# Attention inside a fused attention and two-MoE kernel: projections by float32 matmuls of 64 rows in place of float32r matmuls of a split chunk

## The chip, the cores and the metric

The kernel runs as one program on one core of a Trainium2 chip. The metric is the time of one execution on the device, in microseconds (us), lower is better. PE is the matmul engine (PEld its weight loads), DVE the vector engine, ACT the scalar engine, POOL the GpSimd engine, SP the engine whose queue issues the DMAs.

## What is computed

Three stages follow one another. The first is attention with random features; its output is the input of a gated feed-forward layer (moe1), and that one's output goes through a mixture of eight experts with balanced weights (moe2). The change touches the attention alone:

```
batch, n_heads, seq, head_dim = (4, 8, 576, 64);  n_features = 128
scale = 1.0 / np.sqrt(np.sqrt(D));  q_s, k_s = (q * scale, k * scale)
def phi(x):
    proj = np.einsum('bhsd,md->bhsm', x, omega)
    sq = np.sum(x * x, axis=-1, keepdims=True) / 2.0
    h = proj - sq
    h = h - np.max(h, axis=-1, keepdims=True)
    return np.exp(h) / np.sqrt(m)
q_p, k_p = (phi(q_s), phi(k_s))
kv = np.einsum('bhsm,bhsd->bhmd', k_p, v);  z = np.sum(k_p, axis=2)
num = np.einsum('bhsm,bhmd->bhsd', q_p, kv)
den = np.einsum('bhsm,bhm->bhs', q_p, z)[..., None] + 1e-06
return num / den
```

All arrays are float32.

## The kernel before

The attention works on 36 chunks (18 of k, 18 of q, in turn; `chunks` in `attention`), each of eight blocks of 128 tokens of one head. Every chunk comes from memory twice: as `c["x"]`, tokens in the partitions, and as `xt`, the turned chunk, in which partitions 0 to 63 hold one head's 64 dimensions and partitions 64 to 127 another's. A chunk goes through stages, and the table `ORDER` says in which order the stages are written in each step of the loop `for step in range(NCH + 8)` and how many steps after the chunk's number each stage comes. Each engine runs its instructions in the order in which they were written; nothing reorders them later. So a step is one round of the table, in which every engine handles pieces of several chunks.

- `s0`, `s0r`, `s0n`: sum of squares of a chunk: three POOL instructions (L492, L494, L495) into one scratch block `t0[:, 3]`, one reduction on DVE (L501), a scaling on POOL (L507) to `nsq`. The scratch block is single, so the squares of the next chunk wait for the reduction of this one.
- `s1a`, `s1b`: the turned chunk is split in a high float32r part (ACT, L477) and a low one (DVE, L481).
- `s2p`: the projection on PE. The weights `bdh`, `bdl` are block diagonal, so that one matmul of 128 rows and 256 columns gives two heads; with the split it takes three matmuls (L529, L530, L531) for each of four blocks, 12 for a chunk, into two PSUM banks.
- `s2m`, `s2b`, `s2c`: on DVE the maxima, one reduction for each of the two banks (L536), then two small instructions of 128x8, `hm` (L540) and `bi` (L544).
- `s2x`: on ACT eight exponentials of 128x128 (L551).
- `s3`, `s3a`: for a k chunk, kv and z by ten float32 matmuls of 66 columns (L566, L567), copied out by ACT (L580); for a q chunk eight transposes (L571), copied out by ACT (L584).
- `s4`, `s4d`, `s4r`, `s4n`: q chunks only: eight float32 matmuls of 66 columns (L600; for the tails of the sequence 16 of 64 rows of output, L598), and on DVE denominator (L612), reciprocal (L617) and product (L622).
- `s5`, `s5a`, `s5b`: q chunks only: four transposes (L632), then the output as a high part (ACT, L643) and a low part (DVE, L648).
- `pump`: one piece of the conversion of moe1's first weights (on DVE, POOL and ACT), two pieces in a step.

PSUM has eight banks; `RINGS` says which banks a use takes in turn. In the attention `tr3` has banks 0 and 3, and `tr5`, `pr` and `nu` share six banks. `moe1` is a generator of which each step from NCH + 2 = 38 on takes one piece, so that its matmuls begin in step 38, while the attention's last stages drain. From there on the rings are `DRAIN`.

Of the kernel before, what the change touches and what calls it, by code (L numbers as in the profile page):

```python
# [50 lines left out]
class Kernel:  # L51
    def __init__(self, tc, x, v, vt, omega, wg, wv, wo, w2g, w1, w2, out):
# [10 lines left out]
    ORDER = [("s3a0", 4), ("s0r", 0), ("s5a", 8), ("s2p0", 2), ("s1a", 1), ("s2m0", 2), ("s2p1", 2), ("s40", 5),  # L63
# [3 lines left out]
    RINGS = dict(tr3=(0, 3), tr5=(4, 5, 6, 7, 2, 1), pr=(4, 5, 6, 7, 2, 1), nu=(4, 5, 6,  # L67
                 7, 2, 1), a=(0, 1, 2, 3), b=(4, 5, 6, 7))

    DRAIN = dict(RINGS, tr3=(4, 5), tr5=(4, 5), nu=(6, 7))  # L70

# [289 lines left out]
    def run(self):  # L361
        tc, nc = self.tc, self.nc
        with ExitStack() as ctx:
# [7 lines left out]
            upper = ExitStack()  # L371
            psum = upper.enter_context(tc.tile_pool(name="upper", bufs=1, space=PSUM))
            self.banks += [psum.tile([P, 512], F32, tag=f"b{i}", name=f"bank{i}") for i in range(4, 8)]
# [12 lines left out]
            with tc.manual_schedule():  # L386
                m1 = self.moe1()
                self.attention(m1)
                for _ in m1:
                    pass  # L390
                rest = self.moe2()
                upper.close()
# [6 lines left out]
    def attention(self, m1):  # L399
        tc, nc = self.tc, self.nc  # L400
        if True:
# [7 lines left out]
            t6 = af.tile([P, 2, 2, M], F32R, tag="t6", name="at6")  # L409
# [7 lines left out]
            om2 = t3[:, 0, 0:M]  # L417
            bdh, bdl = t6[:, 0], t6[:, 1]
            nc.gpsimd.memset(f(t6), 0.0)
# [7 lines left out]
            xts = [bx[:, i * 512:(i + 1) * 512] for i in range(4)]  # L427

# [15 lines left out]
            def load(i):  # L444
# [6 lines left out]
                for w, t in ((1, xt), (0, t0[:, k])):  # L451
# [16 lines left out]

            def s1(i):
                c = st[i]  # L470
                k = turn("xT", 4)
                c["xh"], c["xl"] = [self.ar2[:, (x * 4 + k) * 512:(x * 4 + k + 1) * 512].rearrange("p (a t) -> p a t", t=P) for x in range(2)]
                c["tr"] = c["xt"].rearrange("p (a t) -> p a t", t=P)

            def s1a(i):
                c = st[i]
                nc.scalar.copy(c["xh"], c["tr"])  # L477

            def s1b(i):
                c = st[i]  # L480
                nc.vector.tensor_tensor(c["xl"], c["tr"], f(c["xh"]), op=ALU.subtract)  # L481
# [28 lines left out]
            def s2(i):  # L510
# [4 lines left out]
                else:  # L515
                    e = t1[:, turn("e", 2)].rearrange("p (a m) -> p a m", m=M)
                c["e"] = e
                mx = sm.tile([P, 8], F32, tag="mx", name=f"mx{i}", bufs=4)
                hm = sm.tile([P, 8], F32, tag="hm", name=f"hm{i}", bufs=4)
                bi = sm.tile([P, 8], F32, tag="bi", name=f"bi{i}", bufs=4)  # L520
                c["mx"], c["hm"], c["bi"], c["pr"] = mx, hm, bi, []

            def s2p(i, u):
                c = st[i]
                xh, xl = c["xh"], c["xl"]
                pr = self.bank("pr", 2, 2 * M)
                for w in range(2):
                    a = 2 * u + w
# [3 lines left out]
                c["pr"].append(pr)  # L532

            def s2m(i, u):
                c = st[i]
                nc.vector.reduce_max(c["mx"][:, 4 * u:4 * u + 4], c["pr"][u].rearrange("p w (h m) -> p (w h) m", m=M), axis=AX.X)  # L536

            def s2b(i):
                c = st[i]
                nc.vector.scalar_tensor_tensor(c["hm"], c["mx"], SCALE, c["nsq"], op0=ALU.mult, op1=ALU.add)  # L540
# [5 lines left out]
            def s2x(i, u):  # L546
                c = st[i]
                e, bi = c["e"], c["bi"]
                for a in range(4 * u, 4 * u + 4):
                    pr = c["pr"][a // 4].rearrange("p w (h m) -> p (w h) m", m=M)  # L550
                    nc.scalar.activation(e[:, a, :], pr[:, a % 4, :], AF.Exp, bias=bi[:, a:a + 1], scale=SCALE)  # L551
# [100 lines left out]
            fns = dict(s0=s0, s0r=s0r, s0n=s0n, s1=s1, s1a=s1a, s1b=s1b, s2=s2, s2b=s2b, s2c=s2c, s4r=s4r, s5=s5, s5a=s5a, s5b=s5b, pump=pump)  # L652
            halves = dict(s2p=s2p, s2m=s2m, s2x=s2x, s3=s3, s3a=s3a, s4=s4, s4d=s4d, s4n=s4n)
# [11 lines left out]
            for h in range(2):  # L665
                r = slice(h * D, (h + 1) * D)
                nc.scalar.copy(bdh[r, h, :], om2[r])
# [886 lines left out]
```

## Time and profile before

| | |
|---|---|
| time of the runs, median (lowest to highest of 3) | 2108.16 us (2104.68 to 2111.72) |
| the profiled execution: own time given as the span from first to last instruction | 2106.0 us |
| PE busy in the span | 2059.6 us (98%) |
| DVE busy | 1401.3 us (67%) |
| POOL busy | 1053.9 us (50%) |
| ACT busy | 825.8 us (39%) |
| mean granted clock of TensorE | 0.996 |

Busy times are sums over the whole program. Matmuls are pipelined and their ends are modelled, so a PE that reads as busy is not PE at its peak; the distance from the start of one instruction to the start of the next tells more. The program has stages with different limits, and the attention is only the first 180 us of it, so the shares above say little about it. Which of the listed runs was the profiled one is not recorded.

### The profile page before, as it was taken

What the parts mean: (1) busy time and instruction counts of PE and PEld (TensorE: products, weight loads), DVE (VectorE), ACT (ScalarE), POOL (GpSimd) and SP (SyncE); (2) the same over time, 40 slices, a digit from 0 to 9 for tenths busy, and PEclk for the clock granted to TensorE, in tenths of its full rate; (3) what the DMA queues carried; (4) which work ended last, traced back from release to release, by engine and by line L of the source; (5) the groups of instructions that cost most, each with busy time, mean ns of one, the idle gap of its engine ahead of it and who ended that gap; (6) DMA issues with size and microseconds to landing.
All of it is one profiled execution on the core that took longest, in us unless ns stands there. A gap on an engine that the chain in (4) does not pass through costs nothing.

```text
span 2106.0 us, 32639 instructions
## 1 busy us (share of the span) xinstructions
PE 2059.6 (98%) x11836; PEld 1997.4 (95%) x11836; DVE 1401.3 (67%) x2321; ACT 825.8 (39%) x1843; POOL 1053.9 (50%) x1047
## 2 busy tenths in 40 slices
PE   7899999999999999999999999999999999999998
PEld 6889999999998889989888999999999999999998
DVE  6997678778755645445445666666688666666666
ACT  6786433333334444334333423323233433323322
POOL 6783656656533455455652543434454543443443
PEclk9999999999999999999999999999999999999999
DMA  6552556555424656766768788777888887887784
GB/s 203 162 162 77 179 165 197 172 182 176 136 85 157 235 216 228 267 228 246 267 228 303 249 258 264 260 258 251 297 264 267 273 263 258 261 264 253 247 274 153
DMA packets 238130, 467.78 MB, mean 222 GB/s; under 512 B 20272, under 2 KB 110096, under 8 KB 233872
## 3 DMA queue, kind: packets, MB, share of 16 engines
q1 hardware_dynamic: 237968, 465.68, 66.7%
q8 instruction: 94, 1.54, 0.3%
q14 instruction: 68, 0.56, 0.1%
HBM read 340.25 MB, written 125.35 MB: 221 GB/s over the span
## 4 chain that ended last, share of the span: by engine, by line
PE 90%; DVE 7%; POOL 1%; issue 1%; DMA 1%; ACT 0%; SPq 0%; DVEq 0%; POOLq 0%; ACTq 0%
PE bank L1079 13%; PE bank L1325 7%; PE bank L1327 7%; PE bank L1326 7%; PE pair L1416 7%; PE pair L1418 7%; PE pair L1417 7%; PE bank L723 5%; PE bank L725 5%; PE bank L724 5%; PE bank L1020 4%; PE bank L1022 4%; PE bank L1021 3%; PE bank L755 2%; PE bank L757 2%; PE bank L756 2%
## 5 line engine op out<-in xcount | busy, mean ns | idle before, releaser
L1428 DVE TENSOR_TENSOR sums<-pair,sums 128x768 f32<-128x768 f32 x209 | 198.8, 951 | 44.3 <-PE pair L1418 44.3
L1325 PE MATMUL bank<-xh,ar 128*128 128x384 f32 x564 | 188.7, 335 | 2.4 <-ACT mt L1358 2.1
L1327 PE MATMUL bank<-xh,ar 128*128 128x384 f32 x564 | 188.4, 334 | 0.0
L1326 PE MATMUL bank<-xl,ar 128*128 128x384 f32 x564 | 188.4, 334 | 0.0
L1095 DVE SCALAR_TENSOR_TENSOR ac<-bank,mt,ac 128x512 f32<-128x512 f32 x84 | 63.1, 751 | 131.2 <-PE bank L1079 129.3
L1416 PE MATMUL pair<-xh,ar 128*128 128x384 f32 x344 | 115.0, 334 | 0.2 <-DVE sums L1428 0.2
L1418 PE MATMUL pair<-xh,ar 128*128 128x384 f32 x344 | 114.9, 334 | 0.0
L1417 PE MATMUL pair<-xl,ar 128*128 128x384 f32 x344 | 114.9, 334 | 0.0
L1325 PEld LDWEIGHTS bank<-xh,ar 128*128 128x128 f32 x564 | 105.9, 188 | 3.4 <-ACT mt L1358 2.7
L1326 PEld LDWEIGHTS bank<-xl,ar 128*128 128x128 f32 x564 | 105.9, 188 | 0.0
L1327 PEld LDWEIGHTS bank<-xh,ar 128*128 128x128 f32 x564 | 105.9, 188 | 0.0
L737 ACT CAST ar<-mt 128x384 fp32r<-128x384 f32 x72 | 37.0, 514 | 172.6 <-DVE mt L734 172.6
L723 PE MATMUL bank<-xh,ar 128*128 128x384 f32 x288 | 96.6, 336 | 0.0
L725 PE MATMUL bank<-xh,ar 128*128 128x384 f32 x288 | 96.2, 334 | 0.0
L725 PE MATMUL bank<-xh,ar1b 128*128 128x384 f32 x288 | 96.2, 334 | 0.0
L724 PE MATMUL bank<-xl,ar 128*128 128x384 f32 x288 | 96.2, 334 | 0.0
L723 PE MATMUL bank<-xh,ar1b 128*128 128x384 f32 x288 | 96.2, 334 | 0.0
L724 PE MATMUL bank<-xl,ar1b 128*128 128x384 f32 x288 | 96.2, 334 | 0.0
L551 ACT ACTIVATE at<-bank,bi 128x128 f32<-128x128 f32 x288 | 78.4, 383 | 44.5 <-DVE bi L544 34.6
L1020 PE MATMUL bank<-xh,ar 128*128 128x384 f32 x264 | 89.4, 339 | 3.3 <-DVE st L1054 2.5
L1022 PE MATMUL bank<-xh,ar 128*128 128x384 f32 x264 | 88.9, 337 | 0.6 <-DVE ar L265 0.5
L1021 PE MATMUL bank<-xl,ar 128*128 128x384 f32 x264 | 88.5, 335 | 0.0
(382 smaller groups left out, 6932.4 us busy)
## 6 DMA issues: line engine op xcount, KB each, us to landing
ar<-w2forms SPq DMA_DIRECT2D x144, 512.0 KB, 4.4
ar<-w1forms SPq DMA_DIRECT2D x141, 512.0 KB, 4.8
ar1b<-w1forms SPq DMA_DIRECT2D x62, 512.0 KB, 4.8
ar1b<-w2forms SPq DMA_DIRECT2D x61, 512.0 KB, 4.4
w2forms<-ar SPq DMA_DIRECT2D x224, 128.0 KB, 4.1
w1forms<-ar SPq DMA_DIRECT2D x22, 1280.0 KB, 7.0
sumsraw<-in_w_dram SPq DMA_DIRECT2D x32, 512.0 KB, 4.6
w2forms<-sumsraw SPq DMA_DIRECT2D x128, 128.0 KB, 2.8
```

Of the source, the lines that this page charges most:

```text
L723: nc.tensor.matmul(t, hi[:, c, fs], self.xh[:, c, cs], start=(c == 0), stop=False)
L724: nc.tensor.matmul(t, hi[:, c, fs], self.xl[:, c, cs], start=False, stop=False)
L725: nc.tensor.matmul(t, lo[:, c, fs], self.xh[:, c, cs], start=False, stop=(c == KC - 1))
L1020: nc.tensor.matmul(g, ah[:, c, :], bh[:, c, :], start=(first and c == 0), stop=False, skip_group_check=not first)
L1079: nc.tensor.matmul(y, a, w[:, fi % 2, ds], start=(first and x == 0 and k == 0 and fi == fis[0]), stop=(last and x == 1 and fi == fis[-1]))
L1325: nc.tensor.matmul(g, w[:, 0, d], bh[:, d, :], start=bool(first and d == 0), stop=False, skip_group_check=not first)
L1326: nc.tensor.matmul(g, w[:, 0, d], bl[:, d, :], start=False, stop=False, skip_group_check=not first)
L1327: nc.tensor.matmul(g, w[:, 1, d], bh[:, d, :], start=False, stop=(d == 1), skip_group_check=not first)
L1416: nc.tensor.matmul(y, w[:, k, 0, ds], h, start=(k == 0), stop=False)
L1417: nc.tensor.matmul(y, w[:, k, 0, ds], l, start=False, stop=False)
L1418: nc.tensor.matmul(y, w[:, k, 1, ds], h, start=False, stop=(k == 1))
L1428: v.tensor_tensor(a[n], pair, a[n], op=ALU.add)
```

## The change

The turned chunk is no longer split, and `s1`, `s1a`, `s1b` with their tiles are gone. The projection reads `xt` directly as float32: for each of four blocks two matmuls of 64 rows (one head in partitions 0 to 63, one in 64 to 127) and 128 columns, which write to two different banks of one wide PSUM tile. The first attention rings shrink: four banks are the two wide tiles, `tr3` and `tr5` share banks 0 and 3, `nu` has banks 1 and 2. The maxima of a chunk are one reduction over 1024 columns. Exponentials go to four buffers in place of two. The table is rewritten: the stages `s2*` come one step after a chunk's number instead of two, `s5a` and `s5b` seven instead of eight, `s5` six instead of seven, and the loop is one step shorter. The two loads of a chunk are issued in the other order. At step 38 the wide tiles are given up and four single banks take their place.

```diff
-    ORDER = [("s3a0", 4), ("s0r", 0), ("s5a", 8), ("s2p0", 2), ("s1a", 1), ("s2m0", 2), ("s2p1", 2), ("s40", 5),
...
+    ORDER = [("s5a", 7), ("s3a0", 4), ("s2p", 1), ("s5b", 7), ("s2m", 1), ("s40", 5), ("s0r", 0), ("s3a1", 4),
+             ("s2b", 1), ("s4d0", 5), ("s2c", 1), ("s0", -1), ("s30", 3), ("s31", 3), ("s2x0", 1), ("s41", 5),
...
+    RINGS = dict(tr3=(0, 3), tr5=(0, 3), nu=(1, 2), a=(0, 1, 2, 3), b=(4, 5, 6, 7))
...
+            self.twos = [psum.tile([P, 1024], F32, tag=f"b{i}", name=f"two{i}") for i in range(2)]
...
-                for w, t in ((1, xt), (0, t0[:, k])):
+                for w, t in ((0, t0[:, k]), (1, xt)):
...
-            def s1a(i):
-                c = st[i]
-                nc.scalar.copy(c["xh"], c["tr"])
...
-                nc.vector.tensor_tensor(c["xl"], c["tr"], f(c["xh"]), op=ALU.subtract)
...
+                pr = c["pr"] = self.twos[turn("pr", 2)].rearrange("p (w a m) -> p w a m", w=2, m=M)
+                xt = c["xt"].rearrange("p (a t) -> p a t", t=P)
+                for a in range(4):
+                    for w in range(2):
+                        r = slice(w * D, (w + 1) * D)
+                        nc.tensor.matmul(pr[:, w, a, :], xt[r, a, :], om2[r, :], start=True, stop=True)
...
-                    nc.tensor.matmul(pr[:, w, :], xh[:, a, :], bdh, start=True, stop=False)
-                    nc.tensor.matmul(pr[:, w, :], xh[:, a, :], bdl, start=False, stop=False)
-                    nc.tensor.matmul(pr[:, w, :], xl[:, a, :], bdh, start=False, stop=True)
...
+                nc.vector.reduce_max(c["mx"], c["pr"].rearrange("p w a m -> p (w a) m"), axis=AX.X)
...
-            for step in range(NCH + 8):
+            for step in range(NCH + 7):
```

How the rows of an engine move. First PE, in one step in which a q chunk is at `s4`: the end of its projection and the rest of the step, before (`bank_` numbers are PSUM banks, `ar` holds the split, `at` attention's tiles):

```order
L529 MATMUL bank_78<-at_102,ar_62 128x256
L530 MATMUL bank_78<-at_102,ar_62 128x256
L531 MATMUL bank_78<-at_102,ar_62 128x256
L600 MATMUL bank_79<-at_101,at_98 128x66 x4
L571 MATMUL bank_69<-ident,at_97 128x128 x4
L571 MATMUL bank_72<-ident,at_97 128x128 x4
L600 MATMUL bank_71<-at_101,at_98 128x66 x4
L632 MATMUL bank_70<-ident,at_99 128x128 x4
```

And such a step with the change, with the first rows of the next (`two_` is a wide tile, `turned` the chunk as it was loaded, `om` the features):

```order
L509 MATMUL two_76<-om_100,turned 128x128 x8
L578 MATMUL bank_71<-at_99,at_96 128x66 x4
L549 MATMUL bank_72<-ident,at_95 128x128 x4
L549 MATMUL bank_69<-ident,at_95 128x128 x4
L578 MATMUL bank_70<-at_99,at_96 128x66 x4
L509 MATMUL two_77<-om_100,turned 128x128 x8
```

The twelve float32r rows of a projection have become eight float32 rows of half the columns; the other rows are the same ones, and the output's four transposes have moved to the steps of the other parity, where the k chunk's matmuls stand.

Second DVE, one such step before, from the denominator to the output's low part (`nsq` and `ssq` come from and go to POOL):

```order
L612 TENSOR_SCALAR den_1273<-bank_79 128x4
L617 RECIPROCAL rec_1274<-den_1273 128x8
L622 TENSOR_TENSOR at_99<-bank_78,rec_1274 128x4x64
L622 TENSOR_TENSOR at_99<-bank_79,rec_1274 128x4x64
L501 TENSOR_REDUCE ssq_1253<-at_96 128x8
L536 TENSOR_REDUCE mx_1258<-bank_70 128x4
L536 TENSOR_REDUCE mx_1258<-bank_76 128x4
L540 SCALAR_TENSOR_TENSOR hm_1259<-mx_1258,nsq_1220 128x8
L544 SCALAR_TENSOR_TENSOR bi_1260<-hm_1259,nsq_1220 128x8
L481 TENSOR_TENSOR ar_62<-turned,ar_62 128x512
L648 TENSOR_TENSOR xl<-bank_71,xh 128x512
```

And with the change:

```order
L626 TENSOR_TENSOR xl<-bank_72,xh 128x512
L513 TENSOR_REDUCE mx_1220<-two_76 128x8
L485 TENSOR_REDUCE ssq_1189<-at_94 128x8
L519 SCALAR_TENSOR_TENSOR hm_1221<-mx_1220,nsq_1206 128x8
L590 TENSOR_SCALAR den_1244<-bank_71 128x4
L523 SCALAR_TENSOR_TENSOR bi_1222<-hm_1221,nsq_1206 128x8
L590 TENSOR_SCALAR den_1244<-bank_70 128x4
L595 RECIPROCAL rec_1245<-den_1244 128x8
L600 TENSOR_TENSOR at_97<-bank_71,rec_1245 128x4x64
L600 TENSOR_TENSOR at_97<-bank_70,rec_1245 128x4x64
```

The low part of the split is gone, the two maxima are one, and `hm` and `bi` now follow the reduction of the squares (`ssq`) directly, where two maxima stood between them. The output's low part stands first in its step.

## Rows read from the trace of the kernel before

**Rows 1.** Busy time by stretch: us, each engine's busy us (count), PEclk, DMA share, GB/s.
```profile
92.00:138.00 46.00, 41.37 (x354) 39.15 (x353) 44.28 (x100) 36.45 (x113) 36.40 (x46) 0.96 0.52 161
138.00:165.00 27.00, 25.18 (x215) 24.18 (x213) 25.78 (x59) 21.36 (x66) 21.33 (x29) 1.00 0.61 191
180.00:195.00 15.00, 15.00 (x124) 14.62 (x123) 8.37 (x21) 7.18 (x14) 4.33 (x5) 1.00 0.00 1
```
**Rows 2.** Who waited for whom, 40 to 160 us: total us, times, longest us.
```profile
ACT at L551 <- DVE bi L544: 19.1, 20, 1.9
POOL at L492 <- DVE ssq L501: 18.3, 12, 2.1
...
PE bank L531 <- DVE ar L481: 7.7, 10, 1.6
```
**Rows 3.** The instructions of line 540, whole program.
```profile
L540 DVE SCALAR_TENSOR_TENSOR hm<-mx,nsq x36: 166/696/850, 14.0 to 175.9; 128x8 f32<-128x8 f32 x36
```
**Rows 4.** Groups of DVE instructions, 24 to 165 us.
```profile
L536 DVE TENSOR_REDUCE mx<-bank 128x4 f32<-128x512 f32 x60 | 39.2, 682 | 5.3 <-PE bank L531 5.2
L481 DVE TENSOR_TENSOR ar<-turned,ar 128x512 fp32r<-128x512 f32 x31 | 29.8, 963 | 0.0
L540 DVE SCALAR_TENSOR_TENSOR hm<-mx,nsq 128x8 f32<-128x8 f32 x30 | 17.5, 582 | 1.0
...
L544 DVE SCALAR_TENSOR_TENSOR bi<-hm,nsq 128x8 f32<-128x8 f32 x30 | 8.2, 272 | 1.0
```
**Rows 5.** Instructions in order of time, DVE and POOL, one step.
```profile
97.04 0.28 DVE L501 TENSOR_REDUCE ssq<-at 128x8 f32<-128x128 f32 x1
...
97.40 1.04 POOL L492 TENSOR_TENSOR at<-at 128x512 f32<-128x512 f32 x1 [1.61 <-DVE ssq L501]
98.52 0.73 POOL L494 TENSOR_TENSOR at<-at 128x256 f32<-128x256 f32 x1
98.55 0.73 DVE L540 SCALAR_TENSOR_TENSOR hm<-mx,nsq 128x8 f32<-128x8 f32 x1
99.31 0.17 DVE L544 SCALAR_TENSOR_TENSOR bi<-hm,nsq 128x8 f32<-128x8 f32 x1
```
**Rows 6.** In order of time, PE, two steps at the full clock.
```profile
166.84 1.00 PE L600 MATMUL bank<-at,at 128*128 128x66 f32 x8
...
167.68 1.04 PE L571 MATMUL bank<-ident,at 128*128 128x128 f32 x8
...
168.56 1.00 PE L600 MATMUL bank<-at,at 128*128 128x66 f32 x8
...
169.76 0.36 PE L529 MATMUL bank<-at,ar 128*128 128x256 f32 x1
...
171.27 1.00 PE L566 MATMUL bank<-at,at 128*128 128x66 f32 x8
...
173.42 0.37 PE L529 MATMUL bank<-at,ar 128*128 128x256 f32 x1
```
**Rows 7.** In order of time, PE, around a tail chunk.
```profile
111.42 0.28 PE L531 MATMUL bank<-at,ar 128*128 128x256 f32 x1
111.63 0.69 PE L598 MATMUL bank<-at,at 128*64 128x66 f32 x16
112.25 1.09 PE L571 MATMUL bank<-ident,at 128*128 128x128 f32 x8
```
**Rows 8.** In order of time: first squares, first hm, first matmul of moe1.
```profile
8.85 0.45 POOL L495 TENSOR_TENSOR at<-at 128x128 f32<-128x128 f32 x1
...
14.01 0.71 DVE L540 SCALAR_TENSOR_TENSOR hm<-mx,nsq 128x8 f32<-128x8 f32 x1
...
179.59 0.42 PE L723 MATMUL bank<-xh,ar 128*128 128x384 f32 x1
```
**Rows 9.** In order of time, PE, after a wait, at a lower clock.
```profile
100.40 0.58 PE L531 MATMUL bank<-at,ar 128*128 128x256 f32 x1 [1.56 <-DVE ar L481]
...
102.69 1.42 PE L600 MATMUL bank<-at,at 128*128 128x66 f32 x8
```

More of the change, by code (lines that the diff above doesn't have):

```diff
@@ L370, in run @@
             self.banks = [psum.tile([P, 512], F32, tag=f"b{i}", name=f"bank{i}") for i in range(4)]
-            upper = ExitStack()
-            psum = upper.enter_context(tc.tile_pool(name="upper", bufs=1, space=PSUM))
-            self.banks += [psum.tile([P, 512], F32, tag=f"b{i}", name=f"bank{i}") for i in range(4, 8)]
+            self.upper = ExitStack()
+            psum = self.upper.enter_context(tc.tile_pool(name="twos", bufs=1, space=PSUM))
+            self.twos = [psum.tile([P, 1024], F32, tag=f"b{i}", name=f"two{i}") for i in range(2)]
             self.turns, self.rings, self.nquad = {}, self.RINGS, 0
@@ L391, in run @@
                 rest = self.moe2()
-                upper.close()
+                self.upper.close()
                 psum = ctx.enter_context(tc.tile_pool(name="pairs", bufs=1, space=PSUM))
@@ L415, in turn @@
                 return rot[name]
-            om2 = t3[:, 0, 0:M]
-            bdh, bdl = t6[:, 0], t6[:, 1]
-            nc.gpsimd.memset(f(t6), 0.0)
+            om2 = af.tile([P, M], F32, tag="om", name="om2")
             bx = self.cst.tile([P, 6144], F32, tag="ar1b", name="turned")
@@ L427, in attention @@
             xts = [bx[:, i * 512:(i + 1) * 512] for i in range(4)]
+            w = 2048 + 2 * w
+            es = [t1[:, i] for i in range(2)] + [bx[:, w + i * 1024:w + (i + 1) * 1024] for i in range(2)]
             chunks = [("k", 0, None, None)]
@@ L547, in s2x @@
                 c = st[i]
[L548 to L551, printed above, removed]
+                e, bi, pr = c["e"], c["bi"], c["pr"]
+                for n in range(4 * u, 4 * u + 4):
+                    nc.scalar.activation(e[:, n, :], pr[:, n % 2, n // 2, :], AF.Exp, bias=bi[:, n:n + 1], scale=SCALE)
             def s3(i, h):
@@ L651, in attention @@
             pump = lambda i: self.attn_pump()
-            fns = dict(s0=s0, s0r=s0r, s0n=s0n, s1=s1, s1a=s1a, s1b=s1b, s2=s2, s2b=s2b, s2c=s2c, s4r=s4r, s5=s5, s5a=s5a, s5b=s5b, pump=pump)
-            halves = dict(s2p=s2p, s2m=s2m, s2x=s2x, s3=s3, s3a=s3a, s4=s4, s4d=s4d, s4n=s4n)
+            fns = dict(s0=s0, s0r=s0r, s0n=s0n, s2p=s2p, s2m=s2m, s2b=s2b, s2c=s2c, s4r=s4r, s5=s5, s5a=s5a, s5b=s5b, pump=pump)
+            halves = dict(s2x=s2x, s3=s3, s3a=s3a, s4=s4, s4d=s4d, s4n=s4n)
             def stage(n):
@@ L664, in attention @@
             load(1)
-            for h in range(2):
-                r = slice(h * D, (h + 1) * D)
-                nc.scalar.copy(bdh[r, h, :], om2[r])
-                nc.vector.tensor_tensor(bdl[r, h, :], om2[r], f(bdh[r, h, :]), op=ALU.subtract)
             s0(0)
-            for step in range(NCH + 8):
+            for step in range(NCH + 7):
                 if step == NCH + 2:
                     self.rings = self.DRAIN
+                    self.upper.close()
+                    psum = self.upper.enter_context(tc.tile_pool(name="upper", bufs=1, space=PSUM))
+                    self.banks += [psum.tile([P, 512], F32, tag=f"b{i}", name=f"bank{i}") for i in range(4, 8)]
                 if step + 2 < NCH:
```

38 lines of the change are left out of this document (11 added, 27 removed), and 3 rows, old and new, of the table ORDER.

## The prediction

> **What bounds the kernel now.** I read the busy time by stretch first, because the shares over the whole span hide the attention. From 180 us on PE is busy without a gap (15.00 of 15 us) and everything else has room [rows 1]. What the attention saves there arrives at the end in full: moe1's matmuls simply begin earlier. So the only question is when moe1 begins, now at 179.59 us [rows 8].
>
> In the attention DVE is the fullest engine: 44.28 of 46 us and 25.78 of 27 us, while PE reads 41.37 and 25.18, ACT 36.45 and POOL 36.40 [rows 1]. The waits agree: ACT waits for DVE's `bi`, POOL for DVE's `ssq`, and PE for DVE's low part of the split [rows 2]. One `hm` is written per step. The first starts at 14.0 us, the last at 175.9, so 35 steps take 161.9 us, 4.63 us each [rows 3]. DVE is busy 70.06 us of the 73 us of rows 1, which are 15.8 steps: 4.44 us busy and 0.19 idle in each.
>
> **The change on DVE.**
> - The low part of the split goes: 0.96 us a step [rows 4].
> - Two maxima of 682 ns each become one over twice the columns [rows 4]. No row shows 1024 columns. Bounds: 0 to 0.25 us saved; I take 0.10, for one fixed part.
> - `hm` and `bi` change places with the maxima. `ssq` starts at 97.04 and POOL answers with L492 at 97.40 [rows 5]. `hm` starts at 98.55, just behind the start of L494 at 98.52, and both end together (99.28 and 99.25): a 128x8 instruction that elsewhere takes 166 ns [rows 3] lasts 730 ns because POOL is reading. With the change `hm` would start 0.20 us behind `ssq` (where the maximum started), ahead of L492, and take 0.17 us. `bi` would then meet L492 and end with it: 98.44 + 0.17 = 98.61. From the end of the pitch of `ssq` (97.24) that is 1.37 us for the pair, against 0.58 + 0.27 = 0.85 now [rows 4]: 0.52 us lost. In every second step one denominator hides in that time, 0.06 us a step back.
>
> The Trainium skill, page "SBUF — State Buffer", section "Who interferes with whom", states that a DVE instruction with two SBUF inputs and a GpSimd instruction that reads SBUF exclude one another and the second one blocks until the first ends; rows 5 agree. Without the rule, with `hm` and `bi` at their present means, DVE would save 1.06 us a step and not 0.60.
>
> Sum for DVE: 0.96 + 0.10 - 0.52 + 0.06 = 0.60 us less, so 3.84 us busy a step.
>
> **The change on PE.** What stays, at the full clock: a q chunk's step from 166.84 to 169.76, 2.92 us; a k chunk's matmuls from 171.27 to 173.42, 2.15 us [rows 6]; a mean of 2.54 us a step. The projection from 169.76 to 171.27 takes 1.51 us for 12 instructions [rows 6], so PE has 4.05 us of work in a step of 4.63.
>
> The new projection has no row. Each float32 matmul leaves two records (four L600 of the order are eight in the trace), so there are 16 a chunk. The nearest full-height record of 128 columns is the transpose L571, 8 in 0.88 us, 110 ns [rows 6]. One after another, 16 take 1.76 us; in perfect pairs 0.88. The nearest row for two groups of the array at once is L598, half of the columns each: 16 records in 0.62 us, 39 ns [rows 7]. The full width takes 105 ns (8 L600 in 0.84 us [rows 6]), so half the width alone would be about 52 (my estimate, half of it), and side by side they gain a factor of 0.74. I take 16 x 110 x 0.74 = 1.30 us. At the change of shape the trace loses time: L598 starts 0.21 us behind L531 where the pitch is 0.126 [rows 6, 7]; two such changes a step, 0.17 us. PE: 2.54 + 1.30 + 0.17 = 4.01 us, between 3.59 and 4.47.
>
> **The rest.** ACT loses a 128x512 cast a step and POOL nothing; POOL's 36.40 of 46 us [rows 1] are 3.7 us a step, under 4.01, so POOL stays hidden, but only just. The swapped loads are the same bytes, two steps ahead. Four exponential buffers, smaller rings and the wide tiles cost nothing by themselves: the exponentials that free a wide tile end within the next step, and its successor needs it two steps later. With less cover the next thing to be late would be `nu`'s bank, which DVE frees at the end of a q step and a k chunk needs one projection (1.30 us) later.
>
> **The sum.** The fullest engine is now PE with 4.01 us, DVE close behind. I add 0.17 us for waiting, a little under today's idle of DVE, because the two wait for each other: 4.18 us a step. The first `hm` no longer waits a step for the split; it needs the second chunk's squares, which end at 8.85 + 0.45 = 9.30 us [rows 8], and `ssq`, so 9.6 us. 35 steps later comes the last one, in step 36; moe1 still begins in step 38, so a step without projection follows, 2.92 us plus a little, 3.2. Together 9.6 + 3.2 + 35 x 4.18 = 159.1 us, which stands where 175.9 stands now: 16.8 us less. The profiled span of 2106.0 becomes 2089.2; the median of the runs is 2.2 us above that span, so the time is **2091 us**. About 0.3%, 6.3 us, is what a measurement of this kernel can tell from no change.
>
> **Rivals.**
> - **Heads one behind the other.** If the two row halves don't run side by side, the projection is 1.76 us, PE 4.47 and the step 4.64: 12.8 + 162.4 = 175.2 us, 0.7 less, 2107.5 us, no change. Against it: the half-width records [rows 7] do run together. For it: both records of one head are adjacent, so only neighbours of different heads can overlap. The Trainium skill, page "TensorE: Matmul & The Clock Gate", Part 3, "The mechanism", says that a weight load overlaps running matmuls only where the row group differs; eight records of one head at 105 ns load plus 110 ns matmul would make 1.72 us by that rule. Rows 6 speak against it as a general rule, for the full-height transposes keep a pitch of 110 ns, load included. Chance 0.15.
> - **Pairs are perfect and the block vanishes.** If the pairs are perfect, PE has 3.59 us, and if POOL runs late enough that `hm` and `bi` fall into its gaps, DVE has 4.44 - 0.96 - 0.10 - 0.41 - 0.10 = 2.87. Then the step is 3.76: 12.8 + 131.6 = 144.4, 31.5 us less, 2077 us. For it: PE no longer waits for the split [rows 2]. Against it: POOL's 3.7 us. Chance 0.17.
> - **The clock falls: slower.** After a wait of 1.56 us the projection's instructions come every 0.21 us (11 in 2.29 us [rows 9]) in place of 0.126: the lower of the two levels, 1.2 GHz; the stretch's mean is 0.96 [rows 1]. A step of PE then is 8.0 us and the bound, 3.8 us over 4.18. If the half-height matmuls leave the array so idle that the low level lasts, every such step costs that; from 4.4 of them the gain of 16.8 is gone, and twelve make 46 us, 29 us slower, 2137 us. For it: the start of the kernel and the places behind waits. Against it: a slow PE is a full PE, and the wait that let the clock fall most, for the split, is gone. Chance 0.08.
>
> **How the numbers follow.** My forecast has 0.60; its own range by the bounds above is a step of 4.0 to 4.4, 2084.5 to 2099. The 8-in-10 range takes in the no-change rival and most of the faster one: 2075 to 2108. Faster by over 0.3% is the forecast but for a sliver (0.59) and the second rival (0.17): 0.76. Within 0.3% is the first rival but for 0.02, and the sliver: 0.14. Slower is the clock and what is left of the first rival: 0.10.
>
> **What would show it.** Right: the new projection's 16 records take 1.1 to 1.5 us a chunk, every second one starting close behind its neighbour; `hm` takes near 0.17 us and `bi` near 1 us, ending with POOL's first square of the step; PE and DVE both read above 90%; moe1's first matmul starts near 163 us and everything behind it is unchanged. Wrong: 1.7 us or more for the projection; a step far from 4.2 us between the first and last `hm`; a granted clock well below 0.96 in the attention; or a shift in moe1 or moe2, which I hold untouched.

## The result and the profile after

The changed kernel takes 2126.3 us (median of four runs, 2120.8 to 2129.1) against 2109.9 us: a ratio of 1.0083, 95% interval 1.0061 to 1.0105, slower. The forecast was 2091 us. The profiled execution has a span of 2122.6 us, 16.6 above that of before (2106.0).

The place is the one expected. The first matmul of moe1 starts at 196.01 us where it started at 179.59 [rows 8], 16.4 us later, and PE is busy without a gap behind it, as before [rows 1]: moe1 and moe2 are untouched.

```profile
196.01 0.42 PE L700 MATMUL bank<-xh,ar 128*128 128x384 f32 x1
```

Busy time by stretch, after (columns as in rows 1: us, PE, PEld, DVE, ACT, POOL, granted clock, DMA share, GB/s):

```profile
54.00:94.61 40.61, 32.41 (x322) 29.13 (x322) 29.99 (x63) 25.41 (x83) 27.64 (x38) 1.00 0.49 161
60.00:80.00 20.00, 16.66 (x169) 14.83 (x165) 15.71 (x33) 12.91 (x43) 12.72 (x19) 1.00 0.53 173
92.00:138.00 46.00, 38.81 (x325) 34.87 (x326) 34.23 (x72) 26.15 (x85) 27.34 (x38) 0.80 0.46 149
138.00:165.00 27.00, 27.00 (x152) 25.20 (x152) 15.51 (x33) 13.07 (x42) 12.10 (x18) 0.50 0.36 111
200.00:215.00 15.00, 15.00 (x116) 14.65 (x116) 9.53 (x22) 5.69 (x12) 6.84 (x8) 1.00 0.00 1
```

The reader is to see two things. At the full clock (60 to 80 us) no engine is full: PE 83%, DVE 79%, where DVE had 96% [rows 1]. And from 138 to 165 us PE is full at half the clock, where the same stretch of before had 1.00 [rows 1]. The first line spans eight whole steps, from one `hm` to another, all at the full clock: 5.08 us a step, of which PE is busy 4.05 and DVE 3.75.

The instructions of `hm` (line 519) and `bi` (line 523) over the whole program, and groups of DVE from 24 to 165 us (busy us, mean ns, then idle before):

```profile
L519 DVE SCALAR_TENSOR_TENSOR hm<-mx,nsq x36: 154/160/812, 8.6 to 188.6; 128x8 f32<-128x8 f32 x36
```
```profile
L523 DVE SCALAR_TENSOR_TENSOR bi<-hm,nsq x36: 166/1028/1036, 8.8 to 188.8; 128x8 f32<-128x8 f32 x36
```
```profile
L513 DVE TENSOR_REDUCE mx<-two 128x8 f32<-128x1024 f32 x27 | 32.9, 1217 | 6.9 <-PE two L509 6.9
...
L626 DVE TENSOR_TENSOR xl<-bank,xh 128x512 fp32r<-128x512 f32 x12 | 8.3, 692 | 29.7 <-ACT xh L621 29.7
```

35 steps take 180.0 us, 5.14 each, against 4.63 [rows 3]. `hm` fell to 160 ns and `bi` rose to 1028 ns, as forecast. New is the 29.7 us that DVE stands before the output's low part. The same group before, in the same window:

```profile
L648 DVE TENSOR_TENSOR xl<-bank,xh 128x512 fp32r<-128x512 f32 x12 | 8.1, 678 | 0.0
```

The waits from 40 to 160 us (total us, times, longest) say the same:

```profile
POOL at L476 <- DVE hm L519: 42.5, 19, 4.6
DVE xl L626 <- ACT xh L621: 27.8, 11, 3.4
ACT turned L529 <- DVE bi L523: 22.2, 9, 4.1
ACT at L529 <- DVE bi L523: 14.0, 7, 3.1
...
PE bank L549 <- DVE xl L626: 8.8, 7, 1.9
...
PE bank L544 <- DVE at L600: 5.2, 6, 1.0
```

DVE waits for ACT and ACT for DVE: a loop. The instructions in order of time show it over two steps at the full clock:

```profile
64.27 1.04 POOL L476 TENSOR_TENSOR at<-at 128x512 f32<-128x512 f32 x1 [0.90 <-DVE hm L519]
64.30 1.03 DVE L523 SCALAR_TENSOR_TENSOR bi<-hm,nsq 128x8 f32<-128x8 f32 x1
...
65.67 0.76 DVE L600 TENSOR_TENSOR at<-bank,rec 128x256 f32<-128x256 f32 x2
...
66.34 1.22 DVE L513 TENSOR_REDUCE mx<-two 128x8 f32<-128x1024 f32 x1
...
67.86 1.04 DVE L523 SCALAR_TENSOR_TENSOR bi<-hm,nsq 128x8 f32<-128x8 f32 x1
...
69.01 2.20 ACT L529 ACTIVATE at<-two,bi 128x128 f32<-128x128 f32 x8
...
71.03 0.66 ACT L621 CAST xh<-bank 128x512 fp32r<-128x512 f32 x1
...
71.72 0.69 DVE L626 TENSOR_TENSOR xl<-bank,xh 128x512 fp32r<-128x512 f32 x1 [1.60 <-ACT xh L621]
72.33 1.21 DVE L513 TENSOR_REDUCE mx<-two 128x8 f32<-128x1024 f32 x1
...
73.84 1.03 DVE L523 SCALAR_TENSOR_TENSOR bi<-hm,nsq 128x8 f32<-128x8 f32 x1
```

From `bi` to `bi` two steps later is 9.54 us. 4.60 of it is DVE (64.30 to 68.90), 2.82 is ACT (eight exponentials, then the cast that stands behind them on ACT), 2.12 is DVE again. Nothing overlaps in it. This is one of the shorter pairs; the eight steps from 54.00 to 94.61 us make 10.15 us a pair. The first two rows also show the block: `bi` ends with POOL's square (65.33 and 65.31). That agrees with the rule of the Trainium skill, page "SBUF — State Buffer", section "Who interferes with whom", that the prediction drew on.

The low clock. PE in order of time, at its beginning:

```profile
136.39 0.89 PE L549 MATMUL bank<-ident,turned 128*128 128x128 f32 x4 [1.43 <-DVE xl L626]
137.08 1.81 PE L578 MATMUL bank<-at,at 128*128 128x66 f32 x8
138.82 2.08 PE L509 MATMUL two<-om,turned 64*128 64x128 f32 x16
140.83 1.97 PE L544 MATMUL bank<-at,turned 128*128 128x66 f32 x8
```

After a wait of 1.43 us eight records of 66 columns take 1.81 us instead of 1.00 [rows 6] and the projection 2.01 (to the start of line 544's). No wait stands behind, and the low level lasts until 168 us. I count low time in stretches of 4 us, each stretch's length times (1 - granted clock) / 0.5, from 24 us to moe1: 6.9 us before, 51.2 after. It comes from the one profiled execution of each kernel. At the start some traces read 1.00 until the first recorded change although PE runs at the low level's pitch (before: 0.21 us a projection matmul until 29.3 us), so the figure can miss some 5 us, and 6.9 is nearer 12. At the low level PE is the bound, with 7.3 us a step.

### The profile page after: what moved, and what is told of

Same layout as the page of the kernel before. It is cut to its first block, busy times and chain, and to the rows that moved or that the text cites. A ratio compares the mean times of both kernels' runs of the same rounds, so it can differ in the third digit from the quotient of the medians.

```text
span 2122.6 us, 32786 instructions
## 1 busy us (share of the span) xinstructions
PE 2069.0 (97%) x11980; PEld 1999.3 (94%) x11980; DVE 1377.6 (65%) x2247; ACT 806.3 (38%) x1805; POOL 1042.8 (49%) x1046
## 4 chain that ended last, share of the span: by engine, by line
PE 90%; DVE 6%; ACT 2%; issue 1%; POOL 0%; DMA 0%; DVEq 0%; SPq 0%; ACTq 0%; POOLq 0%
PE bank L1056 12%; PE bank L1302 7%; PE bank L1303 7%; PE bank L1304 7%; PE pair L1393 7%; PE pair L1394 7%; PE pair L1395 7%; PE bank L702 5%; PE bank L700 5%; PE bank L701 5%; PE bank L997 3%; PE bank L999 3%; PE bank L998 3%; PE bank L732 2%; PE bank L734 2%; PE bank L733 2%
## 5 line engine op out<-in xcount | busy, mean ns | idle before, releaser
L1056 PE MATMUL bank<-ar,xh 128*128 128x512 f32 x324 | 84.8, 394 | 0.0
```

What stands on the lines that cost most here:

```text
L1056: nc.tensor.matmul(y, a, w[:, fi % 2, ds], start=(first and x == 0 and k == 0 and fi == fis[0]), stop=(last and x == 1 and fi == fis[-1]))
```

## The experiments

All times are medians; ratios are to the kernel before, run on the same chip. "Low" is the low-clock time just defined; "step" the mean from the first to the last `hm`; both are from the profiled execution, which need not be the median run.

### One stage moved in the table

```diff
-             ("s40", 5), ("s0r", 0), ("s3a1", 4), ("s2b", 1), ("s4d0", 5), ("s2c", 1), ("s0", -1),
+             ("s40", 5), ("s3a1", 4), ("s2b", 1), ("s4d0", 5), ("s2c", 1), ("s0r", 0), ("s0", -1),
```

> The changed kernel with the reduction of the squares (ssq) moved behind bi in the table, so that hm and bi run before POOL is set off; nothing else. Theory A (one chain: in every two steps all of DVE's work and, because the output's low part stands first and waits for ACT, 2.7 us of ACT's exponentials and cast stand one behind the other; the pair takes 10.1 us at the full clock): bi falls from 1.03 to 0.17 us, and since it lies in that chain twice a pair, the pair becomes 8.4 us, the step 4.2 in place of 5.14, the attention some 30 us shorter, the time 0.99 of before or less. Theory B (the low clock of PE is what costs, its cause being the half-height matmuls): bi is shorter but the low-clock stretches stay, the step stays at 4.9 or more and the time at 1.005 or more. Theory C (PE waits for banks 0 to 3 set the pace): bi is hidden behind those waits, under 5 us gained.

2111.9 us, 1.0023 (1.0011 to 1.0035); `bi` has a median of 166 ns again, low 52.5 us, step 4.99. The squares that stand ahead of the bias cost some 14 us. That is not all: the step was to be 4.2 by theory A, and the ratio fits none of the three. (The profile is of a run of 2115.5 us, with the lowest mean granted clock of the ten runs, 0.983 against up to 0.991.)

```diff
-             ("s2p", 1), ("s5b", 7), ("s2m", 1), ("s40", 5),
+             ("s2p", 1), ("s2m", 1), ("s40", 5),
...
-             ("s2c", 1), ("s0", -1),
+             ("s2c", 1), ("s5b", 7), ("s0", -1),
```

> The changed kernel with the output's low part (s5b) moved from the head of the step to behind bi; the cast on ACT (s5a) stays first. Theory A: DVE no longer waits for ACT's exponentials of the step before (now 27.8 us in 120), the pair loses up to 2.7 us, but the low part frees the bank that the next transposes need, so PE waits longer there: step 4.4 to 4.7, time 0.995 to 1.002 of before. Theory B: step stays near 5.1, low clock stays. Theory C (bank waits set the pace): the later low part makes it worse than the changed kernel, over 1.01.

2155.6 us, 1.0221 (1.0196 to 1.0246): worse, as theory C had it. DVE's wait for the cast is gone, but the low part now frees the transposes' bank later: PE waits 11.4 us for it (8.8 in the changed kernel), DVE's maxima wait 29.4 us for the projection behind it (3.5), and the clock is low for 126.8 us.

```diff
-    ORDER = [("s5a", 7), ("s3a0", 4), ("s2p", 1), ("s5b", 7), ("s2m", 1), ("s40", 5), ("s0r", 0), ("s3a1", 4),
-             ("s2b", 1), ("s4d0", 5), ("s2c", 1), ("s0", -1),
+    ORDER = [("s3a0", 4), ("s2p", 1), ("s3a1", 4), ("s2m", 1), ("s5", 6), ("s5a", 6), ("s40", 5),
+             ("s2b", 1), ("s2c", 1), ("s0r", 0), ("s4d0", 5), ("s5b", 6), ("s0", -1),
...
```

> The changed kernel with bi before ssq and the output's transposes, cast and low part done one step earlier (transposes just behind the projection in the k step, cast ahead of the exponentials, low part behind bi), so that neither DVE nor PE waits for ACT's exponentials. Theory A: the chain loses both the block of bi (0.86 us a step) and ACT's 2.7 us a pair; the fullest engine is left, PE with 3.6 to 3.8 us or DVE near 3.5: step 3.9 to 4.2, time 0.983 to 0.99 of before, clock at 1.00 throughout. Theory B: low clock stays in the attention, step over 4.7. Theory C: PE still waits for banks, step 4.4 or more.

2120.2 us, 1.0071 (1.0044 to 1.0098); pairs of steps of 8.2 to 8.9 us at the full clock, but 54.6 us of low clock and a new wait, PE for ACT's copies of the transposes (9.6 us), since the output's transposes now want that bank earlier.

### The projection alone, and its heads apart

Before's table and rings, without the split; the float32 projection of 64 rows writes to two banks of the old ring of six.

```diff
-                    nc.tensor.matmul(pr[:, w, :], xh[:, a, :], bdh, start=True, stop=False)
-                    nc.tensor.matmul(pr[:, w, :], xh[:, a, :], bdl, start=False, stop=False)
-                    nc.tensor.matmul(pr[:, w, :], xl[:, a, :], bdh, start=False, stop=True)
+                        nc.tensor.matmul(pr[w][:, a, :], xt[r, a, :], om2[r, :], start=True, stop=True)
```

> The kernel before, its table and rings kept, with only the split taken out and the projection done by float32 matmuls of 64 rows into two banks of the ring (the maxima stay two, one for each bank; a fifth buffer for the turned chunk). Tells the projection from the new table. Theory A (the table is what costs, the projection gains): DVE loses 0.96 us a step and PE 0.3, the step goes from 4.63 to about 4.0, the time is 0.988 to 0.992 of before. Theory B (half-height matmuls bring the low clock): low clock as in the changed kernel, time 1.005 or more. Theory C: near 0.99, as the rings are the old ones.

2099.5 us, 0.9957 (0.9943 to 0.9971): faster than before by 9 us, the only version that computes the whole output and is, though the gain is smaller than theory A's 0.988 to 0.992, and the step longer than its 4.0. Low 17.6 us, step 4.40. A repeat of this kernel, one run, took 2096.5 with 7.6 us of low clock and a step of 4.34. So the arithmetic of the change gains, and the rest of it (table, banks, wide tiles, buffers, order of the loads) loses 27 us.

```diff
-                for a in range(4):
-                    for w in range(2):
+                for w in range(2):
+                    for a in range(4):
```

> The changed kernel with the two loops of the projection exchanged, so that the eight records of one head stand together and only one pair of neighbours differs in its rows. If the two heads of the changed kernel really run side by side (16 records in 1.09 us at the full clock, 68 ns each), the projection becomes 1.7 us or more and PE 0.6 us a step fuller; as PE is not full at the full clock the time rises by 5 to 20 us, mainly through the low-clock stretches, which PE must then cross with more work. If 68 ns is what half the rows cost by themselves, the projection stays at 1.1 us and the time at that of the changed kernel.

2129.0 us, 1.0112 (1.0075 to 1.0149). The 16 records take 1.64 us (62.90 to 64.54), in the changed kernel 1.09 (59.21 to 60.30): neighbours of different heads do run side by side. The changed kernel, then this run:

```profile
59.21 1.16 PE L509 MATMUL two<-om,turned 64*128 64x128 f32 x16
60.30 1.11 PE L578 MATMUL bank<-at,at 128*128 128x66 f32 x8
```
```profile
62.90 1.71 PE L509 MATMUL two<-om,turned 64*128 64x128 f32 x16
64.54 1.11 PE L578 MATMUL bank<-at,at 128*128 128x66 f32 x8
```

The time rises by 3 us, less than the 5 to 20 expected, for PE isn't the bound; low is 29.9 us, less than the 51.2 of the changed kernel.

### The clock held

One full-height float32 matmul of 512 columns, whose result nothing reads, ahead of each projection:

```diff
+                nc.tensor.matmul(pr[:, 0].rearrange("p a m -> p (a m)")[:, 0:512], xt[:, 0, :], c["xt"][:, 0:512], start=True, stop=True)
```

> The changed kernel with one more matmul at the head of each projection, of full height (128 rows) and 512 columns of float32, whose result the projection overwrites: work that is good for nothing, 0.85 us of PE a step at the full clock. Theory B (a mix with half-height matmuls holds the low clock, even where PE has no gap): the low-clock stretches of 51 us in the attention shrink to under 20, and the time falls or stays (2112 to 2126) though PE does more. Theory A alone (waits let the clock fall and nothing else matters): low-clock stretches stay as long and each step in them takes 9 us in place of 7.3, so 2135 or more.

2118.0 us, 1.0044 (1.0030 to 1.0058). PE does 0.95 us more a step, the low clock is 0.0 us, and the kernel is 8 us faster. The step is 4.89. The eight steps that lie in both kernels at the full clock are equally long (40.71 us padded, 54.72 to 95.43, against 40.61), so there the padding costs nothing and PE is not what bounds them.

The same without useless work, four full-height matmuls against a block-diagonal omega:

```diff
-                    for w in range(2):
-                        r = slice(w * D, (w + 1) * D)
-                        nc.tensor.matmul(pr[:, w, a, :], xt[r, a, :], om2[r, :], start=True, stop=True)
+                    nc.tensor.matmul(pr[:, a].rearrange("p w m -> p (w m)"), xt[:, a, :], om2, start=True, stop=True)
```

> The changed kernel with its projection at full height: four float32 matmuls of 128 rows and 256 columns against a block-diagonal omega (zeros off the diagonal) instead of eight of 64 rows and 128 columns; nothing else. It costs PE 0.6 us a step more (the full-height records of 128 columns take 0.105 us, so 16 times that, 1.7 us, against 1.09). Clock theory: the 51 us of low clock go to below 5 although PE waits as often, time 2112 to 2120 (the padded run had 2118.0). Chain theory alone: no difference that the chain sees, 2126 within 4, the low clock where it was. If neither, and PE is the bound: 35 times 0.6 is 21 us more, 2140 to 2150.

2120.6 us, 1.0056 (1.0037 to 1.0075), low 9.5 us, step 4.92: the clock theory, a little outside its ranges (below 5 us, 2112 to 2120). By stretch:

```profile
60.00:80.00 20.00, 18.87 (x134) 16.79 (x133) 15.34 (x32) 12.74 (x43) 13.95 (x20) 1.00 0.55 182
92.00:138.00 46.00, 40.07 (x281) 34.54 (x279) 33.25 (x69) 28.53 (x93) 29.03 (x41) 0.96 0.51 167
138.00:165.00 27.00, 23.77 (x170) 21.28 (x169) 21.47 (x46) 16.12 (x52) 16.40 (x24) 1.00 0.44 138
```

PE and DVE wait as in the changed kernel (PE 9.6 us for the low part, DVE 29.2 us for the cast), yet the clock comes back each time. Both runs give PE more work as well as more rows, so they don't tell the two apart. The run with the heads apart does: its projection is about as long as this one's (1.64 us against 1.73, 62.40 to 64.13), at half height, and low is 29.9 us there and 9.5 here. By these profiles, one of each kernel, the fall from 51.2 goes partly with the longer work and partly with the height. The mean granted clocks of all runs are in the same order (0.977 to 0.985 changed, 0.986 to 0.991 heads apart, 0.994 to 0.995 here). Nor is half height enough by itself, for the projection alone has it too, with 17.6 and 7.6 us. Holding the clock gains 6 to 8 us net of the added work, and at the full clock the step is still 4.9 us, far from 4.18.

### The clock held, and the table changed

> The first experiment (squares' sum behind the bias, 2111.9 us) with the useless full-height matmul ahead of each projection (alone: 2118.0 us). If the two losses are separate (14 us of bias, 8 us of low clock net of the pad's own time) they add: 2102 to 2106, no low clock. If they are the same time counted twice: 2110 to 2114. If the pad's 0.95 us a step makes PE the bound once the chain is shorter: above 2114, with PE without idle time.

The first edit with the padding: 2109.1 us, 1.0008 (0.9995 to 1.0021), low 0.0, step 4.71. Between the two forecasts; the bias is worth 8.9 us here (2118.0 to 2109.1). PE reads 19.1 of 20 us from 20 to 180 us, so the pad may have become a bound; no run shows it.

> The squares' sum behind the bias (alone: 2111.9 us with 52 us of low clock) and the projection at full height (alone: 2120.6 us with 9.5 us of low clock). If the bias's wait and the clock are the whole of the loss, they add: 2126.3 - 14 - 6 = 2106, range 2103 to 2110, low clock below 10 us, and then some 8 us of the difference to the padded pair (2109.1) is PE's idle time given back. If the chain through ACT (cast first, then the low part at the head of DVE's step) is the bound whatever the bias does: DVE's wait for the cast grows above 30 us between 40 and 160 us and the time stays at 2112 or above.

The first edit at full height: 2111.0 us, 1.0015 (1.0005 to 1.0025), low 9.2 us, step 4.63. From 2120.6 the bias gives 9.6 us, and DVE still waits 28.3 us for the cast. The two shown losses add, but to 15 us, not to the 20 forecast, and the time lies between the two forecasts.

> The low part behind the bias (alone: 2155.6 us with 127 us of low clock) and the projection at full height. Clock theory: the low clock goes to below 20 us, and the time falls by more than 30 us, below 2125. Chain theory: DVE no longer waits for the cast at the head of a step, so it comes out below the run with full height alone: 2108 to 2116. Bank theory: the low part holds the transposes' bank longer, PE's waits for it (14 us between 40 and 160 us in the run with the low part later alone) stay, and the time is 2118 to 2128 without low clock.

The second edit at full height: 2143.8 us, 1.0167 (1.0148 to 1.0187), above every theory's range. The clock theory had the direction alone: 30.7 us of low clock where it wanted below 20, and 12 us faster than at half height where it wanted over 30. The step is 5.56, and the waits from 40 to 160 us name the bank:

```profile
PEld bank L544 <- DVE xl L621: 25.8, 10, 4.0
PE bank L544 <- DVE xl L621: 23.4, 10, 3.8
```

Line 544 here is the q chunk's transposes, which share two banks with the output's. Early, the low part waits for ACT; late, PE waits for the low part.

> The run with bias first and the output's split a step earlier (2120.2 us, 55 us of low clock, pairs of steps of 8.6 us at the full clock) with the projection at full height. Chain and clock theory together: low clock below 10 us, pairs of 8.6 to 9.0 us, time 2098 to 2106, the lowest of this table's kernels. If the bank waits (13 us of PE's bank for the output's transposes in that run) or PE's 0.6 us more are the bound: pairs of 9.4 or above, 2110 or above.

The third edit at full height: 2111.1 us, 1.0010 (0.9999 to 1.0021), low 13.7 us, step 4.72. A miss for the loop as I had drawn it, and what its rivals had forecast (2110 or above). DVE's wait for the cast has fallen to 1.4 us, and another wait of the same size stands in its place:

```profile
DVE mx L508 <- PE two L504: 25.0, 17, 5.0
...
DVE xl L621 <- ACT xh L616: 1.4, 2, 1.1
```

### Other banks

```diff
-    RINGS = dict(tr3=(0, 3), tr5=(4, 5, 6, 7, 2, 1), pr=(4, 5, 6, 7, 2, 1), nu=(4, 5, 6, 7, 2, 1),
+    RINGS = dict(tr3=(0, 3), tr5=(0, 3), pr=(4, 5, 6, 7), nu=(1, 2),
```

> The projection alone with before's table, but the change's division of the banks: four banks for the projections, two for kv and numerator, and two shared by both kinds of transposes. Theory C (the small rings make PE wait, and the waits let the clock fall): slower than the projection alone by 10 us or more, 1.002 of before or above, PE waits for DVE's low part and for the numerator's bank. Theory A (order, not banks): within 5 us of the projection alone, 0.993 to 0.998, or faster, as a projection no longer waits for the exponentials of the last one.

The projection alone with the change's banks under before's table: 2086.9 us, 0.9900 (0.9883 to 0.9916), low 4.1 us. This kernel doesn't compute the attention's output: in that order the output's transposes overwrite a bank before the q chunk's transposes are copied from it, and are overwritten before the low part is read. So waits that a usable kernel must have are missing, and its time shows only what these banks would allow without them.

The same with an order in which every bank is read before it is written again:

```diff
+    ORDER = [("s3a0", 4), ("s0r", 0), ("s5a", 7), ("s2p0", 2), ("s2m0", 2), ("s2m1", 2), ("s2b", 2), ("s2c", 2),
+             ("s3a1", 4), ("s40", 5), ("s5b", 7), ("s0", -1), ("pump", 3), ("s2", 1), ("s30", 3), ("s2x0", 2),
+             ("s31", 3), ("s4d0", 5), ("s41", 5), ("s0n", 0), ("s5", 6),
...
+    RINGS = dict(tr3=(0, 3), tr5=(1, 2), pr=(4, 5, 6, 7), nu=(1, 2),
```

> The projection alone (2099.5 us, before's table) with banks of their own: the projections keep 4 to 7, the numerators and the output's transposes share 1 and 2, the transposes keep 0 and 3; the output's transposes one step earlier, its low part behind the bias, the first numerator behind the copies, so that each bank is read before it is written again. If the shared ring was what held the projection alone back: near the run with new rings, 2086 to 2093, low clock below 10 us, steps of 4.1 to 4.2. If the order's new waits (numerator behind the copy, numerator's bank behind the low part) cost what the rings give: 2098 to 2106. Clock theory's rival: 20 us of low clock or more, 2100 or above.

2123.7 us, 1.0073 (1.0044 to 1.0102), low 51.3 us: a miss. With six banks in rotation the projection alone had no wait of PE for this copy; with two, the numerators wait for ACT's copy of a k chunk's sums (line 561), which must leave one of their two banks first:

```profile
DVE den L593 <- PE bank L581: 18.2, 11, 3.1
PEld bank L581 <- ACT at L561: 17.5, 9, 2.3
PE bank L581 <- ACT at L561: 15.8, 9, 2.1
```

The seven runs of this one kernel go from 2112.6 us at a mean granted clock of 0.994 to 2134.3 at 0.975, so the time of the same program moves by 22 us together with its clock. Against a run of the projection alone at the same 0.994 (2094.1 us) the run at 2112.6 is still some 18 us longer: that much goes with the order and the banks, not with the clock.

The changed kernel with the output's transposes in the numerators' pair and a late output:

```diff
+    ORDER = [("s3a0", 4), ("s3a1", 4), ("s2p", 1), ("s2m", 1), ("s5a", 7), ("s2b", 1), ("s2c", 1), ("s0r", 0),
+             ("s5b", 7), ("s0", -1), ("s30", 3), ("s31", 3), ("s2x0", 1), ("s40", 5), ("s4d0", 5), ("s41", 5),
...
-    RINGS = dict(tr3=(0, 3), tr5=(0, 3), nu=(1, 2),
+    RINGS = dict(tr3=(0, 3), tr5=(1, 2), nu=(1, 2),
```

> The changed kernel with another order of a step: the bias ahead of the squares' sum, the output's cast behind the maxima, its low part last before the denominators, the copies of the transposes first; and the output's transposes in the numerators' pair of banks instead of the transposes' pair. Serial chain theory (bias held up by the squares on GpSimd, low part waiting for the cast that stands behind the exponentials): both terms go, the bias takes 0.17 us instead of 1.03, DVE's wait of the low part for the cast (27.8 us between 40 and 160 us) falls below 8, the step goes from 5.14 us to 4.3 to 4.5, time 2098 to 2106. Clock theory (the half-height projections keep the clock low once PE has waited): the low clock still takes 40 us or more before moe1 and the time stays at 2108 or above, whatever the order. Bank theory (PE's waits for the shared banks are what starts it): PE's waits for a bank that the low part holds go to nothing, the low clock falls below 20 us and the time is 2098 to 2106 as well, but with the bias's share alone (14 us, the first experiment) explaining less than half of the step.

2120.7 us, 1.0060 (1.0039 to 1.0080), low 60.6 us, step 5.12, as the clock theory had it (40 us or more, 2108 or above). The cast is no longer waited for; the maxima wait for the projection instead, and the numerators for the low part:

```profile
DVE mx L513 <- PE two L509: 27.2, 12, 5.4
...
PE bank L578 <- DVE xl L626: 9.9, 7, 2.9
```

> Both at once: the order and banks of the run with the output late, and the projection at full height. Chain and clock theory together: low clock below 5 us, step 4.2 to 4.5, time 2092 to 2104, below the run with the output late alone if that one still has over 20 us of low clock, otherwise up to 10 us above it (PE 0.6 us a step more). If PE is the bound by then: 2105 to 2115 with PE idle under a tenth of the time.

The same at full height: 2120.0 us, 1.0056 (1.0038 to 1.0074), low 3.4 us, step 4.80, PE waiting 13.5 us for the low part: above both forecasts. 57 us less of low clock gain 0.7 us here. The maxima still wait 20.5 us for the projection; whether the waits or PE's longer projection take the gain isn't shown.

### The projection a step before its maxima

```diff
+    ORDER = [("s3a0", 4), ("s3a1", 4), ("s2m", 1), ("s40", 5), ("s2b", 1), ("s2c", 1), ("s0r", 0), ("s4d0", 5),
+             ("s0", -1), ("s30", 3), ("s31", 3), ("s2x0", 1), ("s2p", 0), ("s5", 6), ("s41", 5), ("s0n", 0),
+             ("pump", 3), ("s5a", 6), ("s2x1", 1), ("s4d1", 5), ("s5b", 6), ("s4r", 5),
...
```

> The changed kernel with its wide tiles and banks, and an order that cuts the loop across the engines: the projection of a chunk one step before its maxima (behind the k and q chunk's matmuls), the bias before the squares' sum, the output's transposes behind the matmuls of the step after its product, its cast between the two halves of the exponentials, its low part behind the denominators. Loop theory (the step is the loop maxima, bias, exponentials, copy or cast, bank, maxima, and no engine is full): DVE's waits for the cast and for the projection go below 8 us each between 40 and 160 us, steps of 4.2 to 4.5, time 2094 to 2106. Clock theory: with the half-height projection over 40 us of low clock stay and the time is 2108 or above. Bank theory (two banks for numerators and transposes are too few in any order): PE's waits for banks stay above 20 us, 2110 or above.

> The same order with the projection at full height (0.6 to 0.85 us of PE a step more). Loop and clock theory together: low clock below 15 us, steps of 4.3 to 4.5 with PE busy over 95 % of the time, 2096 to 2106, and below the half-height one of this order if that shows over 30 us of low clock. Bank theory: 2110 or above.

2145.4 us, 1.0177 (1.0156 to 1.0198), low 96.9 us, at half height; 2122.9 us, 1.0067 (1.0051 to 1.0083), low 17.0 us, at full height. Both are above the loop theory's ranges. The same table, and 22 us between them, the most that the height of the projection makes in any of the six orders that were run at both heights (0.7 to 12 us in the others). No maximum waits for PE any more, as expected, but DVE waits 39.7 and 33.0 us for the cast, because the cast waits on PE for the output's transposes (22.5 and 16.4 us) behind a k chunk's matmuls and a projection. The loop was not cut but led through PE.

## Why the prediction was wrong

- **The terms of the two engines held.** The projection takes 1.09 us (forecast 1.30, bounds 0.88 to 1.76), so the heads do run in pairs. PE at the full clock is busy 4.05 us a step (32.41 us in the eight steps from 54.00 to 94.61), forecast 4.01, and DVE 3.75, forecast 3.84. `bi` takes 1.03 us and ends with POOL, forecast near 1; the maxima 1217 ns, two of before 1364 [rows 4], so 0.15 us saved where 0.10 was taken. The first `hm` starts at 8.64, forecast 9.6. moe1 and moe2 are untouched. moe1 starts 33.2 us later than forecast (196.01 against 162.8), and the 35 steps alone are 33.7 longer (180.0 against 146.3); the start and the tail give 0.5 us back.
- **The step that failed is "I add 0.17 us for waiting".** It read the idle of the fullest engine in a kernel with one full engine (0.19 us of DVE) as the price of waiting in one where none is. The wait at the full clock is 1.0 us in those eight steps (5.08 - 4.05), and the whole attention with the clock held has steps of 4.89 and 4.92, 0.9 over the 4.01. Its two sources stand in the record as harmless. The bias's block was counted as DVE time only, where DVE had room; it lies on the loop from `bi` through the exponentials back to `bi`, and costs 9 to 14 us. And "smaller rings and the wide tiles cost nothing by themselves" was checked for the wide tiles alone. With two banks each for the transposes with the output and for the numerators, the output's low part is either early, and waits for a cast that stands behind the exponentials, or late, and holds a bank for which PE waits: 23 us more between the runs at full height that differ in that alone (2120.6 and 2143.8). The prediction named `nu`'s bank as the next to be late, and it is (PE waits 5.2 us for it in the changed kernel); the transposes' bank, which it didn't name, costs more (8.8).
- **The rival "the clock falls" came about, by a mechanism near the one given.** After a wait for DVE's low part the low level lasts with the half-height projection, and hardly at full height or padded. How much of that is the height and how much the added work of PE rests on the run with the heads apart (29.9 us low against 9.5 at full height). It was given 0.08, since "the wait that let the clock fall most, for the split, is gone"; other waits took its place. Its price per step was 3.8 us over 4.18; a low step measures 7.3 us. But it doesn't carry the slowdown alone: with the clock held the kernel is still 9 to 12 us slower than before (1.0044 and 1.0056).
- **The sum, measured.** Forecast to result is 35 us. The clock is 6 to 8, net of the work that held it, the bias 9 to 10 at a held clock (14 at half height). The remaining 17 to 20 us answer to the step that is left with the bias first and the clock held, 4.63 at full height and 4.71 with the padding, 0.45 to 0.53 us above 4.18, times 35. The projection alone under the old table has 4.40 (4.34 in its repeat), so some 0.2 us of that rest may be an estimate that was too low for the old table as well; that the other half comes with the new banks or order is argued, not shown.
- **What stays open.** Whether an order exists in which the change's banks are no loss. Five rearrangements (the second and third edit, the numerators' pair, the old table with narrow rings, the early projection) moved the wait (cast, maxima, transposes' bank, numerators' bank, cast through PE) and none reached 2099.5. That two-bank rings are the reason is the reading that fits all of them, above all old table with narrow rings (2123.7) against six banks in rotation (2099.5), 18 us apart at a like clock; but that run moved stages as well, so the banks by themselves aren't shown to be it.

## What to carry to other kernels

When a change empties the fullest engine, don't put the next engine's busy time plus a little idle as the new step: draw the loop that an item goes through (here maxima, bias, exponentials, cast, low part, bank, maxima) and add it up with the in-order queues on it, for it bounds the step when no engine does. Take an arithmetic change and a change of buffers and order apart before pricing them: here the first gained 9 us and the second lost 27. A wait that costs little by itself can cost more by what it does to PE's clock, so look, beside the waits, at the mix of matmuls with which PE resumes.

## What the runs showed of the hardware

- The low level of the clock can outlast its cause by far with PE without idle time: 27.00 of 27 us busy at a granted 0.50 here, with float32 matmuls of which those of the projection fill half the rows. With 0.95 us of full-height matmul more a step it did not fall once behind 24 us, and the kernel was 8 us faster for doing more. With some 0.55 us more a step at half height low was 29.9 us, with 0.64 more at full height 9.5.
- Two heads in the two halves of the rows, alternating, take 68 ns a record (1.09 us for 16); the same records one head after the other take 103 (1.64 us).
